# Chunk-selected attention with a gated MLP: score tiles of two PSUM banks, and one shared PSUM pool

## The chip, the core and the metric

The kernel runs on one core of one Trainium2 chip. The metric is device time in microseconds, the median of several executions. The engines are TensorE (PE, with PEld for its weight loads), VectorE (DVE), ScalarE (ACT), GpSimd (POOL) and SyncE (SP, which here only issues DMAs). PE writes to PSUM, a memory of eight banks; a bank holds 512 float32 columns on 128 partitions. ACT and DVE read PSUM out.

## What is computed

Four batches, eight heads, 768 positions, head dimension 64. For each query the keys are grouped into 24 chunks of 32. An upper bound of the query's score with each chunk comes from the chunk's smallest and largest key values; the six chunks with the highest bounds are kept. Masked softmax attention follows, and its output feeds an MLP with a spatial gate:

```python
k_min, k_max = np.min(k_chunks, axis=3), np.max(k_chunks, axis=3)
ub = np.sum(np.maximum(q[..., None, :] * k_min, q[..., None, :] * k_max), axis=-1)   # shapes left out
top_chunks = np.argsort(np.where(causal, ub, -1e9), axis=-1)[..., -6:]
scores = scale * np.matmul(q, k.transpose(0, 1, 3, 2))
scores = np.where(sel & causal_by_position, scores, -1e9)
attn = softmax(scores);  x = attn @ v            # then heads are joined: (4, 768, 512)
h = np.maximum(x @ w_in, 0.0);  u, v = h[..., :512], h[..., 512:]
v_n = (v - mean(v)) / np.sqrt(var(v) + 1e-06)
gated = u * (w_spatial @ v_n + b_spatial)
out = gated @ w_out
```

## The kernel before

**Units of work.** Two heads form a pair; there are 16 pairs, four to a batch. A head's lower triangle of scores, keys on partitions and queries along columns, has 21 blocks of 128 x 128. `TILES` packs them into six tiles of at most 512 columns: five full ones and one of 128. A tile is filled by one or two matmuls (L266), in batch 0 followed by one more that adds the triangular mask to the diagonal block (L269). One ACTIVATE (L271) then turns the tile into exponentials `e`, in float16, with scale and no bias. For batches 1 to 3 the mask is put on afterwards, by POOL, over the six diagonal blocks of the whole head (L278). `values` (L289) multiplies the 21 blocks of `e` with v, which has a column of ones appended, into one accumulator bank; `normalise` (L296, L297) divides by the sum.

**Preparation of a pair.** It happens one to two pairs ahead. PE transposes the keys (`k_transpose`, L170) into a PSUM tile kTp. DVE reduces it to chunk maxima and minima (L178, L182) and copies it into the operand `kh` (L194). kTp stays taken until the second of these copies. The queries are transposed (L205) and split into positive and negative parts `rq` by two DVE instructions (L210, L214). Eleven matmuls (L219, L222) make the bounds `ub`. Ten MAX8 instructions (L232) and one comparison (L237) turn them into selection columns, written beside the queries; `ub` stays taken until the comparison. The queries with these columns are transposed once more (L251), copied out by ACT or, early on, by DVE (L257), for the first eight pairs. For the later ones a DMA transposes them.

**The MLP.** It works on one batch while the next one's attention runs. Groups of four or six matmuls of 512 columns (L388) fill one bank each: 24 groups v, read by ACT (L398) and followed by statistics (L400) and a normalisation (L412) on DVE; 24 groups u, read by ACT (L420); 24 groups s, read by DVE (L427); 24 groups o, read by ACT (L437) and stored. Six transposed tiles of w_spatial, wtr, are copied out once by DVE (L369).

**Banks.** All eight are given out: three to the pool `ps_sc` (score tiles), one to `ps_tr`, one to `ps_acc` (the accumulator of `values`), three to `ps_ml`. `ps_ml` holds MLP groups, kTp and wtr, and in batch 0, when no MLP runs yet, the transposes of queries, selections and attention output (trm in the profile). In later batches these transposes go to `ps_tr` (tr in the profile). `ub` is always in `ps_tr`.

**Order.** A table of beats, twelve to a pair, lists which step comes when. The functions are called in that order, and the language's scheduler fixes each engine's queue from it, the data and the free buffers. Each engine then runs its own queue strictly in order. An instruction that waits for a semaphore holds up all that stand behind it on its engine. Only about the first pair and a half are ordered by hand on PE.

Of the kernel before, what the change touches and what calls it, by code (L numbers as in the profile page):

```python
# [10 lines left out]
F32 = mybir.dt.float32  # L11
F16 = mybir.dt.float16
Alu = mybir.AluOpType
Act = mybir.ActivationFunctionType
AX = mybir.AxisListType

P = 128
# [6 lines left out]
TILES = [  # L24
    [(0, 0, 512, 0)],
    [(1, 128, 512, 0)],
    [(2, 256, 512, 0)],
    [(3, 384, 384, 0), (1, 640, 128, 384)],
    [(4, 512, 256, 0), (0, 512, 256, 256)],
    [(5, 640, 128, 0)],  # L30
]
# [17 lines left out]
def kernel(  # L49
# [11 lines left out]
    nc = tc.nc  # L61
    B, H, S, D = q.shape
# [10 lines left out]
    scale = 1.0 / math.sqrt(D)  # L73
    mm = nc.tensor.matmul
# [2 lines left out]
    ring = ctx.enter_context(tc.tile_pool(name="ring", bufs=1))  # L77
    sb = ctx.enter_context(tc.tile_pool(name="sb", bufs=2))
    ml = ctx.enter_context(tc.tile_pool(name="ml", bufs=2))
    ps_sc = ctx.enter_context(tc.psum_pool(name="ps_sc", bufs=3))  # L80
    ps_tr = ctx.enter_context(tc.psum_pool(name="ps_tr", bufs=1))
    ps_acc = ctx.enter_context(tc.psum_pool(name="ps_acc", bufs=1))
    ps_ml = ctx.enter_context(tc.psum_pool(name="ps_ml", bufs=3))

# [11 lines left out]
    def at(beat, fn, *args):  # L96
        beats[beat].append((fn, args))
# [9 lines left out]
    identity = cp.tile([P, P], F16)  # L107
    tri = cp.tile([P, P], F16)
# [48 lines left out]
    class Pair:  # L157
# [37 lines left out]

        def trans_tile(self):

            if self.b == 0:
                return ps_ml.tile([P, S], F16, tag="mlp", name="trm")
            return ps_tr.tile([P, S], F16, tag="tr", name="tr")  # L200

        def q_transpose(self):
            self.tr = self.trans_tile()
# [11 lines left out]
                                        op0=Alu.mult, op1=Alu.max)  # L215

        def bounds(self):
            ub = self.ub = ps_tr.tile([P, 512], F32, tag="tr", name="ub")
            mm(ub[:, 0:(NQT - 1) * W], lhsT=sub_chunk, rhs=later, start=True, stop=False)  # L219
            for qi in range(1, NQT):  # L220
                for m in range(2):
                    mm(ub[:, (qi - 1) * W:qi * W], lhsT=self.rq[:, m, qi * P:(qi + 1) * P],  # L222
                       rhs=self.km[:, m].rearrange("p h c -> p (h c)"), start=False, stop=(m == 1 and qi == NQT - 1))
# [36 lines left out]
        def scores(self, hi, g):  # L260
            if g == 0:
                self.e[hi] = sb.tile([P, EW], F16, tag="e", name="e", bufs=3)
            self.sc = sc = ps_sc.tile([P, 512], F32, tag="sc", name="sc")
            for si, (t, q0, n, col) in enumerate(TILES[g]):
                diag = self.b == 0 and si == 0
                mm(sc[:, col:col + n], lhsT=self.kh[hi][:, t * P:(t + 1) * P],  # L266
                   rhs=self.a[:, q0 // P:(q0 + n) // P, hi, :], start=True, stop=not diag)
                if diag:
                    mm(sc[:, 0:P], lhsT=identity, rhs=tri, start=False, stop=True)  # L269
            width = sum(n for (_, _, n, _) in TILES[g])  # L270
            nc.scalar.activation(out=self.e[hi][:, g * 512:g * 512 + width], in_=sc[:, 0:width], func=Act.Exp, scale=scale)  # L271

        def triangle(self, hi):
            if self.b == 0:
# [198 lines left out]
    for g in range(1, NPAIR // 2):  # L473
        t0 = 2 * g * BEATS
# [4 lines left out]
    for i, p in enumerate(pairs):  # L479
        t0 = i * BEATS  # L480
        for hi in range(2):
            for g in range(len(TILES)):
                at(t0 + 6 * hi + g, p.scores, hi, g)
            at(t0 + 6 * hi + 6, p.triangle, hi)
            at(t0 + 6 * hi + 6, p.values, hi, LOWER[0], True)
            at(t0 + 6 * hi + 8, p.values, hi, LOWER[1])
            at(t0 + 6 * hi + 10, p.values, hi, DIAG, False, True)
            at(t0 + 6 * hi + 11, p.normalise, hi)
        at(t0 + 18, p.x_transpose)
    for i, p in enumerate(pairs):  # L490
        t0 = i * BEATS
# [20 lines left out]
    p, n = pairs[0:2]  # L512
# [82 lines left out]
```

## Time and profile before

Three runs took 208.97, 209.21 and 209.23 us; the median is 209.21. The profiled span is 206.9 us, with the TensorE clock granted in full throughout.

| what | before |
|---|---|
| ACTIVATE e<-sc, 128x512 | 160, mean 605 ns |
| ACTIVATE e<-sc, 128x128 | 32, mean 290 ns |
| MATMUL mlp, 128x512 | 432, mean 379 ns |
| MATMUL sc, all widths | 256, and 48 mask matmuls |
| MATMUL acc, 128x65 | 672, mean 193 ns |
| first matmul, last matmul | 5.7 us, 202.6 us |
| first exponential, last exponential | 15.3 us, 167.1 us |
| first MLP matmul | 55.1 us |

Matmuls are pipelined: the mean of one is the time from its start to its modelled end, while the next one starts much earlier. A row that says "x24" with a duration covers a run of neighbours, and from such rows the distance of two starts can be had. Busy shares of ACT and DVE are sums of the time in which at least one of the engine's instructions was under way. In tables of stretches a line gives the busy time and the number of instructions of PE, PEld, DVE, ACT and POOL in this order. In lists of waits the three numbers are the total in us, how many times, and the longest.

### The profile page before, as it was taken

The numbers are of one execution on the slowest core, as the hardware profiler recorded it, in microseconds if no ns is written. First come the engines' busy times: TensorE is split into PE (matmuls) and PEld (weight loads), VectorE is DVE, ScalarE is ACT, GpSimd is POOL, SyncE is SP. The second block draws the span as 40 slices with busy tenths as digits, with TensorE's granted clock in tenths as the row PEclk, the third lists the DMA queues.
The fourth block names the chain that finished last, engine by engine and source line by source line (L and its number), as shares of the span: only waits on it lengthen the run. The fifth ranks groups of instructions, "written<-read, shape, count | busy, mean of one in ns | idle before, by whom it ended". The sixth has DMA issues, their size and how long they took to land.

```text
span 206.9 us, 5068 instructions
## 1 busy us (share of the span) xinstructions
PE 187.8 (91%) x1922; PEld 115.1 (56%) x1922; DVE 154.5 (75%) x454; ACT 158.1 (76%) x326; POOL 80.5 (39%) x100
## 2 busy tenths in 40 slices
PE   0368999898899999999999999999999999999992
PEld 0266776775666665656655656565555454444440
DVE  6467979989799989899797999887647456365520
ACT  4797989899998889785989996669999830666042
POOL 7997659596992463236114111111111110000000
PEclk9999999999999999999999999999999999999999
DMA  5999999999999999979998926648782124540356
GB/s 38 92 118 154 140 178 158 173 177 167 177 162 162 97 119 128 135 130 147 149 278 153 180 62 57 127 88 158 181 166 65 38 29 92 187 152 3 72 128 256
DMA packets 114424, 27.27 MB, mean 132 GB/s; under 512 B 109536, under 2 KB 110816, under 8 KB 114400
## 3 DMA queue, kind: packets, MB, share of 16 engines
q0 software_dynamic: 76544, 12.20, 89.8%
q1 hardware_dynamic: 37856, 14.75, 36.4%
q8 instruction: 15, 0.25, 0.5%
q14 instruction: 9, 0.07, 0.1%
HBM read 24.38 MB, written 6.29 MB: 148 GB/s over the span
## 4 chain that ended last, share of the span: by engine, by line
PE 69%; ACT 17%; DVE 8%; issue 2%; DMA 2%; POOL 0%; DVEq 0%; ACTq 0%; POOLq 0%
PE mlp L388 40%; PE sc L266 12%; ACT e L271 10%; PE acc L289 7%; PE kTp L170 2%; ACT a L257 2%; DVE kmm L178 2%; PE ub L222 2%; DMA k<-in_k_dram 2%; PE trm L251 2%; ACT vraw L398 1%; PE tr L205 1%; DVE vn L412 1%; DVE kmm L182 1%; ACT u L420 1%
## 5 line engine op out<-in xcount | busy, mean ns | idle before, releaser
L271 ACT ACTIVATE e<-sc 128x512 f16<-128x512 f32 x192 | 96.9, 553 | 14.8 <-PE sc L266 13.4
L266 PE MATMUL sc<-a,kh 128*128 128x512 f16 (+3 forms) x256 | 65.5, 308 | 2.1 <-ACT e L271 1.5
L388 PE MATMUL mlp<-w_in_sb,xT 128*128 128x512 f16 x192 | 53.0, 379 | 0.1
L278 POOL TENSOR_SCALAR_AFFINE_SELECT e<-e 128x768 f16<-128x768 f16 x24 | 20.9, 869 | 66.3 <-ACT e L271 66.3
L289 PEld LDWEIGHTS <-e 128*128 128x128 f16 x672 | 31.4, 97 | 17.0 <-DVE x L297 3.8
L388 PE MATMUL mlp<-vn,wsT 128*128 128x512 f16 x144 | 37.3, 379 | 0.0
L289 PE MATMUL acc<-vt,e 128*128 128x65 f16 x672 | 35.3, 193 | 0.7 <-DVE x L297 0.4
L266 PEld LDWEIGHTS <-kh 128*128 128x128 f16 x256 | 22.7, 98 | 13.3 <-issue 0.8
L437 ACT COPY o<-mlp 128x512 f32<-128x512 f32 x24 | 14.1, 586 | 19.5 <-PE mlp L388 19.1
L400 DVE BATCH_NORM_STATS2 stats<-vraw 128x6 f32<-128x512 f32 x24 | 16.6, 693 | 12.9 <-ACT vraw L398 12.5
L388 PE MATMUL mlp<-w_out_sb,gT 128*128 128x512 f16 x96 | 25.1, 379 | 0.0
L388 PEld LDWEIGHTS <-xT 128*128 128x128 f16 x192 | 17.2, 97 | 12.6 <-issue 0.4
L427 DVE SCALAR_TENSOR_TENSOR g<-mlp,b_col,u 128x512 f16<-128x512 f32 x24 | 17.9, 748 | 7.3 <-PE mlp L388 6.2
L232 DVE MAX8 max<-ub 128x8 f32<-128x8 f32 (+4 forms) x160 | 15.6, 165 | 5.1 <-PE ub L222 4.9
L388 PEld LDWEIGHTS <-wsT 128*128 128x128 f16 x144 | 12.9, 98 | 10.4
L178 DVE TENSOR_REDUCE kmm<-kTp 128x24 f16<-128x768 f16 x16 | 15.2, 948 | 3.7 <-PE kTp L170 2.7
L297 DVE TENSOR_TENSOR x<-acc,rec 128x384 f16<-128x384 f32 x32 | 17.6, 551 | 0.4
L336 POOL DMA_DIRECT2D qs<-in_q_dram x14 | 14.6, 1049 | 5.9 <-PE sc L266 5.9
L194 DVE COPY kh<-kTp 64x768 f16<-64x768 f16 x30 | 16.5, 549 | 0.5
L398 ACT ACTIVATE vraw<-mlp 128x512 f32<-128x512 f32 x24 | 14.4, 601 | 3.0 <-PE mlp L388 3.0
L420 ACT ACTIVATE u<-mlp 128x512 f16<-128x512 f32 x24 | 14.3, 598 | 1.7 <-PE mlp L388 1.5
L327 POOL DMA_DIRECT2D k<-in_k_dram x14 | 14.4, 1045 | 2.5 <-PE kTp L170 1.8
(67 smaller groups left out, 230.2 us busy)
## 6 DMA issues: line engine op xcount, KB each, us to landing
out_dram<-o SPq DMA_DIRECT2D x24, 256.0 KB, 2.3
vt<-in_v_dram POOLq DMA_DIRECT2D x8, 384.0 KB, 8.8
k<-in_k_dram POOLq DMA_DIRECT2D x14, 192.0 KB, 8.1
qs<-in_q_dram POOLq DMA_DIRECT2D x14, 192.0 KB, 7.5
ws_raw<-in_moe_w_spatial_dram POOLq DMA_DIRECT2D x6, 192.0 KB, 6.9
w_in_sb<-in_moe_w_in_dram POOLq DMA_DIRECT2D x8, 128.0 KB, 6.9
w_out_sb<-in_moe_w_out_dram POOLq DMA_DIRECT2D x4, 128.0 KB, 7.9
k<-in_k_dram POOLq DMA_DIRECT2D x4, 96.0 KB, 3.4
```

Source lines behind the costliest of these rows:

```text
L178: nc.vector.tensor_reduce(self.kmm[:, 0, :], self.kT.rearrange("d (c ch) -> d c ch", ch=CHUNK), axis=AX.X, op=Alu.max)
L194: copy(self.kh[hi][d0:d1], self.kT[d0:d1])
L266: mm(sc[:, col:col + n], lhsT=self.kh[hi][:, t * P:(t + 1) * P], rhs=self.a[:, q0 // P:(q0 + n) // P, hi, :], start=True, stop=not diag)
L271: nc.scalar.activation(out=self.e[hi][:, g * 512:g * 512 + width], in_=sc[:, 0:width], func=Act.Exp, scale=scale)
L278: nc.gpsimd.affine_select(out=blk, in_=blk, compare_op=Alu.is_ge, fill=0.0, base=0, channel_multiplier=-1, pattern=[[0, NQT], [1, P]])
L289: mm(self.av[:, qi, :], lhsT=self.e[hi][:, c:c + P], rhs=self.v[hi][:, t, 0:D + 1], start=first and n == 0, stop=last and n == len(blocks) ...
L297: nc.vector.tensor_tensor(self.x16[:, :, hi, :], in0=self.av[:, :, 0:D], in1=rec.to_broadcast([P, NQT, D]), op=Alu.mult)
L388: mm(st[group][:, 0:cols], lhsT=lhsT, rhs=rhs, start=(j == 0), stop=(j == n - 1))
L398: nc.scalar.activation(st["vraw"][:, ti, :], h, func=Act.Relu)
L400: nc.vector.bn_stats(stats, st["vraw"][:, ti, :])
L420: nc.scalar.activation(st["u"][:, ti, :], h, func=Act.Relu)
L427: nc.vector.scalar_tensor_tensor(g, in0=vs, scalar=b_col[:, ti:ti + 1], in1=st["u"][:, ti, :], op0=Alu.add, op1=Alu.mult)
```

## The change

The three score banks and the bank of `ps_tr` become two score tiles of two banks each. A score tile takes two neighbouring entries of `TILES`, so that a head has three of 1024, 1024 and 640 columns, and one ACTIVATE reads both banks. The pool `ps_tr` is gone: `ub` and all the transposes take turns in `ps_ml` with kTp, wtr and the MLP. The aim is to issue half as many exponentials, each with one fixed cost, without using more than eight banks. The values matmuls keep their beats; the score tile g is now called at beat 2g of its head instead of g.

```diff
-    ps_sc = ctx.enter_context(tc.psum_pool(name="ps_sc", bufs=3))
-    ps_tr = ctx.enter_context(tc.psum_pool(name="ps_tr", bufs=1))
+    ps_sc = ctx.enter_context(tc.psum_pool(name="ps_sc", bufs=2))
     ps_acc = ctx.enter_context(tc.psum_pool(name="ps_acc", bufs=1))
     ps_ml = ctx.enter_context(tc.psum_pool(name="ps_ml", bufs=3))
...
         def trans_tile(self):
 
-            if self.b == 0:
-                return ps_ml.tile([P, S], F16, tag="mlp", name="trm")
-            return ps_tr.tile([P, S], F16, tag="tr", name="tr")
+            return ps_ml.tile([P, S], F16, tag="mlp", name="trm")
...
         def bounds(self):
-            ub = self.ub = ps_tr.tile([P, 512], F32, tag="tr", name="ub")
+            ub = self.ub = ps_ml.tile([P, 512], F32, tag="mlp", name="ub")
...
         def scores(self, hi, g):
             if g == 0:
                 self.e[hi] = sb.tile([P, EW], F16, tag="e", name="e", bufs=3)
-            self.sc = sc = ps_sc.tile([P, 512], F32, tag="sc", name="sc")
-            for si, (t, q0, n, col) in enumerate(TILES[g]):
-                diag = self.b == 0 and si == 0
-                mm(sc[:, col:col + n], lhsT=self.kh[hi][:, t * P:(t + 1) * P],
-                   rhs=self.a[:, q0 // P:(q0 + n) // P, hi, :], start=True, stop=not diag)
-                if diag:
-                    mm(sc[:, 0:P], lhsT=identity, rhs=tri, start=False, stop=True)
-            width = sum(n for (_, _, n, _) in TILES[g])
-            nc.scalar.activation(out=self.e[hi][:, g * 512:g * 512 + width], in_=sc[:, 0:width], func=Act.Exp, scale=scale)
+            sc = ps_sc.tile([P, 1024], F32, tag="sc", name="sc")
+            width = 0
+            for half, part in enumerate(TILES[2 * g:2 * g + 2]):
+                for si, (t, q0, n, col) in enumerate(part):
+                    col += 512 * half
+                    diag = self.b == 0 and si == 0
+                    mm(sc[:, col:col + n], lhsT=self.kh[hi][:, t * P:(t + 1) * P],
+                       rhs=self.a[:, q0 // P:(q0 + n) // P, hi, :], start=True, stop=not diag)
+                    if diag:
+                        mm(sc[:, col:col + P], lhsT=identity, rhs=tri, start=False, stop=True)
+                    width += n
+            nc.scalar.activation(out=self.e[hi][:, g * 1024:g * 1024 + width], in_=sc[:, 0:width], func=Act.Exp, scale=scale)
...
         for hi in range(2):
-            for g in range(len(TILES)):
-                at(t0 + 6 * hi + g, p.scores, hi, g)
+            for g in range(len(TILES) // 2):
+                at(t0 + 6 * hi + 2 * g, p.scores, hi, g)
```

## The prediction

> **What bounds the kernel now.** I read the page's engine line first, then a table of stretches, the waits, the order of time, and the groups by shape.
>
> ```profile
> PE 187.8 (91%) x1922; PEld 115.1 (56%) x1922; DVE 154.5 (75%) x454; ACT 158.1 (76%) x326; POOL 80.5 (39%) x100
> ```
>
> TensorE leads, but the average hides two regimes. The table of stretches (busy us of PE, PEld, DVE, ACT, POOL) splits them:
>
> ```profile
> 20.00:40.00 20.00, 18.55 (x281) 14.13 (x280) 18.41 (x61) 17.92 (x38) 13.71 (x22) 1.00 2.50 162
> 40.00:60.00 20.00, 17.85 (x257) 13.01 (x256) 17.63 (x56) 19.19 (x43) 17.28 (x21) 1.00 1.92 170
> 60.00:80.00 20.00, 19.39 (x233) 12.85 (x231) 18.99 (x60) 17.45 (x37) 10.72 (x11) 1.00 1.98 130
> 80.00:140.00 60.00, 60.00 (x632) 36.40 (x631) 53.61 (x159) 48.68 (x107) 15.21 (x16) 1.00 1.19 136
> ```
>
> Until about 78 us no engine is full: ACT leads at 40 to 60 (19.2 of 20), DVE at 60 to 80 (19.0), the two are level at 20 to 40. From 80 on PE is full and ACT is not (48.7 of 60). A busy PE need not be at its peak, so I checked its starts. In the timeline four MLP matmuls take 1.03 us and one 0.379, so the pitch is 0.217 us; a transpose's is 0.056, a values matmul's 0.030 (21 take 0.81). By such pitches the gaps between starts sum to 10.0 us from 20 to 80 us, and to 1.1 us from 80 until the end of PE at 203, of which one wait is 0.5. **After 80 us the kernel is TensorE back to back: nothing ACT saves there can shorten it, and each new PE stall there lengthens it one for one.** The waits of PE after 78 us agree; this is the whole list:
>
> ```profile
> PE acc L289 <- DVE x L297: 0.4, 1, 0.4
> ```
>
> By shape, the exponentials (busy, mean ns, idle before):
>
> ```profile
> L271 ACT ACTIVATE e<-sc 128x512 f16<-128x512 f32 x160 | 91.6, 605 | 14.8 <-PE sc L266 13.4 <-PE sc L269 0.7
> L271 ACT ACTIVATE e<-sc 128x128 f16<-128x128 f32 x32 | 9.3, 290 | 0.0
> ```
>
> And how long a bank stays taken after its last matmul, from the timeline:
>
> ```profile
> 197.67 5.34 PE L388 MATMUL mlp<-w_out_sb,gT 128*128 128x512 f16 x24
> ...
> 198.73 0.58 ACT L437 COPY o<-mlp 128x512 f32<-128x512 f32 x1 [8.04 <-PE mlp L388]
> ```
>
> The first group's fourth matmul starts at 197.67 + 3 x 0.217 = 198.32 and its copy ends at 199.31: a lag of 0.99 us on an idle ACT. Taken the same way for all groups from 78 to 166 us, the lag of a bank read by ACT is 1.00 to 1.46 (medians 1.06 to 1.12); read by DVE at L427, 1.17 to 1.92 (median 1.45); a score tile, median 1.02; the bound tile ub, 1.6 to 4.5 (median 2.7); a kT tile, 5.5 to 9.9.
>
> **The Trainium skill.** "ScalarE: Activation LUTs", What ACT_TABLE_LOAD costs: with immediate scale and bias an ACTIVATE costs 186 ns plus 0.833 ns a column, and neighbours overlap by about 93 ns. The trace agrees: (605 - 290) / 384 = 0.82 ns a column and 185 ns fixed; back to back, four take 2.09 us, so the pitch is (2.09 - 0.605) / 3 = 0.495, an overlap of 110 ns. "PSUM — Partial Sum Buffer", The four PSUM rules: one matmul writes at most one bank, so a 1024-column tile still takes two or more matmuls; "Advanced Engine Details and Errata", The Read-Write Bubble: trn2 can read several banks with one instruction. No run here has shown that yet. "Perfetto Trace Analysis", Matmuls: independent groups should rotate through banks so that reading one out overlaps the next. The trace agrees: MLP groups do so without a gap.
>
> **The change, part by part.**
>
> 1. Fewer exponentials. Per head six (five of 512, one of 128) become three (1024, 1024, 640): 192 become 96. Columns stay. What goes is the part of the pitch that isn't columns, 0.495 - 0.82 x 0.512 = 0.075 us, three times a head: 0.225 a head, 7.2 us of ACT in all. (The fixed 185 ns would give 17.8, but 110 of them overlap already.) Matmuls stay 1922, with the same pitches: 0. On the path lies only what falls before 78 us: 85 of the exponentials, 14 heads, at most 14 x 0.225 = 3.2 us. DVE, whose work is unchanged, has 55.0 of 60 us filled from 20 to 80 and is the fuller engine in two of the three rows, so I take 40% of it: **-1.3 us** (bounds 0 and -3.2). The 18 heads after that save 4.1 us of an ACT with 11 us of idle in 80 to 140: 0.
>
> 2. Score buffers: three of one bank become two of two. Two 1024 tiles hold more, but in coarser steps. In batch 0 each half takes a score and a mask matmul, 0.216 + 0.056; two halves plus about 0.4 us until a result is read is 0.95, and the other tile's exponential lasts 0.92 at its pitch. Before, 0.27 + 0.4 stood against two pitches, 0.99. The slack of 0.3 us is gone; any other PE work between halves shows on ACT. This is the second reason for 40%.
>
> 3. Banks. ps_tr's bank goes away; transposes of every batch and ub now share ps_ml's three with kT and the MLP. Mean banks held in before (last reader's end minus first matmul, summed, over the stretch): 20 to 55 us, kT 1.13 + transposes 0.93 + ub 0.57 = 2.63 of four; 55 to 78, MLP 1.10 + kT 1.00 + ub 0.45 + transposes 0.44 + wtr 0.43 = 3.42 of four; 78 to 166, MLP 1.36 + kT 0.49 + ub 0.25 + transposes 0.13 = 2.23. Now three serve. A PE wait on a bank blocks everything behind it in PE's one queue: scores, so ACT, and values, so DVE.
>
> The built order of instructions shows where. For each PE wait I added the PE pitches between the last matmul that its releaser's engine had waited for and the waiting matmul: the time PE can fill before it must stall. The coarse order is the same (at head 32 both have issued 280 of 432 MLP matmuls), but the distances shrink. Between 50 and 140 us of PE work (about 74 to 165 us on the clock), waits on a bank read by ACT with under 1.1 us: **before 1, after 11** (0.83, 0.84, 0.87, 0.88, 0.89, 0.89, 0.98, 1.05, 1.06, 1.08, 1.08). On a bank read at L427 with under 1.35: before 0, after 5 (1.10, 1.22, 1.31, 1.31, 1.33). After an L369 copy: before 1.53, after 0.71 and 0.92. Shortfalls against median lags: ACT at 1.08, 1.4; three of these evictions stand right behind a 1024 exponential, 0.42 longer than before, less what they had to spare, 1.0; L427 at 1.45, 1.0; L369 at 1.25 (its median), 0.9; score tiles, lag 1.02 + 0.42 for 1024 and + 0.10 for 640 columns against 1.01, 1.22 and 0.92, 0.8. Sum 5.1. They aren't wholly additive, since one stall lengthens the next distance and a third stand within 2 us of another; I take three quarters, less the 0.2 that before had there: **+3.7 us** (bounds 0.8 with every lag at its shortest 1.00, and 5.1). As a check the rule on before: its one ACT distance of 0.83 should stall 0.25, and the timeline has a gap of 0.235 there.
>
> 4. The same between 36 and 50 us of PE work (59 to 74 us). ACT distances 0.76, 0.76, 0.83, 0.85, 0.93 against 0.98, 0.98 before: 1.3 - 0.2; L369 distances 0.71, 0.75, 0.85 against 0.73: 1.4 - 0.5. Sum 2.0, but DVE is 19.0 of 20 full there and hides about half: **+1.0 us** (0.3 to 3.2; the upper end is 3.42 - 3 = 0.42 banks too few, 14% of 23 us).
>
> Sum: -1.3 + 3.7 + 1.0 = +3.4, so 209.2 + 3.4 = **212.6 us**. The tail from 166 us on keeps its three MLP banks and distances of 1.94 and more: 0.
>
> **Rivals.** (a) Faster: ACT's saving is real time until 78 us and evictions are prompt: -3.2 + 0.8 + 0.3 gives **207.1**. For it: ACT's 19.2 of 20 at 40 to 60. Against: DVE at 19.0 next to it. (b) A draw: -2 + 1.5 + 0.5, **209.2**. (c) Banks become the bound: nothing gained early, 3.2 lost in 55 to 78 and all 5.1 later: **217.5**. For it: 3.42 banks wanted of three. Against: part of that 3.42 is tiles waiting for a reader.
>
> **Chances.** My forecast 0.5, (a) 0.2, (b) 0.1, (c) 0.2. The range cuts half of (a) and half of (c): 207.2 to 217.0. Forecast and (c) are slower, with a little of (b): 0.71; the draw within 0.2% 0.06; faster 0.23.
>
> **What would show it.** L271: 64 of about 1.02 us and 32 of 0.71, ACT busy down by about 7 to 9 us: part 1. PE waiting for ACT and DVE at L388, L310 and the transposes between 80 and 166, where it had 0.4 us: part 3. ACT idle before 78 us, waiting for L266: part 2. A PE without gaps from 80 on, and an earlier 80, would prove me wrong, and rival (a) right.

## The result and the profile after

The changed kernel takes **215.97 us** (median of five, 215.73 to 218.33) against 209.21 us (five, 208.82 to 209.54): a ratio of 1.0351, 95% interval 1.0306 to 1.0397. That is 6.8 us more, where the prediction said 3.4 more. The direction was right and the time lies in the range; the size was half of what came.

The profiled execution was the slowest of the five, 218.33 us. An unchanged control, `after_again`, was profiled at 216.11 us, and its readings are used unless the first profile is named. Its engine line, and its exponentials by shape (busy us, mean ns, idle before):

```profile
PE 190.7 (89%) x1922; PEld 116.0 (54%) x1922; DVE 155.3 (72%) x454; ACT 151.2 (71%) x230; POOL 81.4 (38%) x100
```

```profile
L271 ACT ACTIVATE e<-sc 128x1024 f16<-128x1024 f32 x64 | 64.2, 1023 | 12.7 <-PE sc L266 9.4 <-PE sc L269 1.6 <-POOL e L278 1.1
L271 ACT ACTIVATE e<-sc 128x640 f16<-128x640 f32 x32 | 22.6, 707 | 8.2 <-PE sc L266 6.6 <-PE sc L269 1.5
```

The change does what it says: 96 exponentials instead of 192, ACT busy for 151.2 us instead of 158.1. But these fewer instructions stand behind 20.9 us of idle ACT (12.7 + 8.2), where before it was 14.8 us. Most of what ACT saved, it waits for. The stretches of the control, in the columns of the prediction's table:

```profile
20.00:40.00 20.00, 17.35 (x270) 13.57 (x269) 17.27 (x57) 16.54 (x22) 13.86 (x22) 1.00 2.49 162
40.00:60.00 20.00, 17.23 (x257) 13.13 (x254) 16.36 (x59) 17.61 (x26) 16.31 (x20) 1.00 1.92 170
60.00:80.00 20.00, 18.57 (x211) 12.06 (x210) 18.25 (x49) 16.32 (x28) 9.90 (x10) 1.00 1.48 116
80.00:140.00 60.00, 58.07 (x590) 34.36 (x589) 51.81 (x156) 43.77 (x69) 16.00 (x18) 1.00 1.12 128
```

PE lost time in every stretch: 18.55 became 17.35 in the first, and the full 60.00 from 80 to 140 us became 58.07. Its matmuls per stretch fell too (632 to 590 in the last). PE's waits from 80 us on, where before had a single one of 0.4 us (total, times, longest), again in the control:

```profile
PE sc L266 <- ACT e L271: 0.7, 2, 0.4
PE mlp L388 <- ACT u L420: 0.6, 3, 0.3
PE sc L266 <- DMA a<-qs: 0.3, 1, 0.3
PE mlp L388 <- ACT o L437: 0.3, 1, 0.3
```

These are the MLP's banks read out by ACT (L420, L437), as the forecast had it, score tiles, and one wait for a DMA that transposes queries (a<-qs). None is long. One of them in the control's timeline (start us, us, instruction, idle before):

```profile
105.76 0.58 ACT L437 COPY o<-mlp 128x512 f32<-128x512 f32 x1
...
106.40 1.02 PE L388 MATMUL mlp<-w_in_sb,xT 128*128 128x512 f16 x4 [0.26 <-ACT o L437]
```

The copy that frees the bank ends at 106.34. The group that needs it starts at 106.40, and PE has stood for 0.26 us. The list of waits holds only the longer ones (1.9 us in all). The sum of all gaps between PE's starts, by the pitches of the prediction, tells the whole:

| PE gaps, us | before 20 us | 20 to 80 | from 80 | last matmul at |
|---|---|---|---|---|
| before | 8.93 | 9.97 | 1.13 | 202.6 |
| control of after | 9.65 | 13.06 | 4.97 | 210.1 |
| difference | +0.7 | +3.1 | +3.8 | +7.5 |

The differences add up to 7.6 us, and the last matmul came 7.5 us later. So the whole loss is PE standing still, half of it before 80 us and half after.

The first profile also had one long wait. Its timeline at 54 us, and the clock line of its page (40 slices of 5.4 us):

```profile
54.33 1.42 POOL L343 DMA_DIRECT2D vt<-in_v_dram  x1 [0.74 <-PE trm L248]
...
55.80 0.86 POOL L278 TENSOR_SCALAR_AFFINE_SELECT e<-e 128x768 f16<-128x768 f16 x1
...
56.72 0.52 PE L289 MATMUL acc<-vt,e 128*128 128x65 f16 x6 [2.15 <-POOL e L278]
```

```profile
PEclk9999999999799999999999999999999999999999
```

GpSimd issues a load of v (L343) before it masks a head's exponentials (L278); the mask starts 1.47 us later, and PE waits 2.15 us for it. In before the two stood the other way round (the mask at 52.93, the load at 53.74). The clock fell in the same slice. In the control the same wait is 0.5 us and the clock stays at 1.00, and its time is 2.2 us shorter. Hence all but 0.5 us of this wait is part of the slowest execution, not of the 6.8 us.

### The profile page after: what moved, and what is told of

The parts are those of the page before. It is cut to its first block, busy times and chain, and to the rows that moved or that the text cites. A ratio compares the mean times of both kernels' runs of the same rounds, so it can differ in the third digit from the quotient of the medians.

```text
span 216.6 us, 4975 instructions
## 1 busy us (share of the span) xinstructions
PE 191.4 (88%) x1922; PEld 116.0 (54%) x1922; DVE 155.2 (72%) x454; ACT 151.2 (70%) x230; POOL 81.4 (38%) x100
## 4 chain that ended last, share of the span: by engine, by line
PE 67%; ACT 15%; DVE 6%; DMA 5%; issue 3%; POOL 3%; POOLq 0%; ACTq 0%; DVEq 0%
PE mlp L388 41%; PE sc L266 11%; ACT e L271 10%; PE acc L289 6%; DMA a<-qs 3%; PE kTp L169 2%; DMA qs<-in_q_dram 2%; PE ub L219 2%; PE trm L248 2%; PE trm L202 1%; ACT u L420 1%; DVE kmm L177 1%; ACT vraw L398 1%; ACT a L254 1%; DVE kmm L181 1%
## 5 line engine op out<-in xcount | busy, mean ns | idle before, releaser
L271 ACT ACTIVATE e<-sc 128x1024 f16<-128x1024 f32 (+1 forms) x96 | 85.6, 918 | 23.1 <-PE sc L266 18.2
L266 PE MATMUL sc<-a,kh 128*128 128x512 f16 (+3 forms) x256 | 55.8, 309 | 4.2 <-ACT e L271 3.4
L388 PE MATMUL mlp<-w_in_sb,xT 128*128 128x512 f16 x192 | 50.6, 380 | 1.2 <-ACT vraw L398 0.4
L278 POOL TENSOR_SCALAR_AFFINE_SELECT e<-e 128x768 f16<-128x768 f16 x24 | 21.0, 874 | 66.9 <-ACT e L271 66.8
L289 PEld LDWEIGHTS <-e 128*128 128x128 f16 x672 | 30.6, 98 | 17.2 <-DVE x L297 2.5
L388 PE MATMUL mlp<-vn,wsT 128*128 128x512 f16 x144 | 35.6, 379 | 0.3 <-ACT u L420 0.3
L437 ACT COPY o<-mlp 128x512 f32<-128x512 f32 x24 | 14.0, 585 | 21.8 <-PE mlp L388 21.3
L266 PEld LDWEIGHTS <-kh 128*128 128x128 f16 x256 | 21.8, 98 | 12.7 <-issue 3.6
L388 PEld LDWEIGHTS <-xT 128*128 128x128 f16 x192 | 17.7, 98 | 18.5 <-issue 3.6
L388 PE MATMUL mlp<-w_out_sb,gT 128*128 128x512 f16 x96 | 24.1, 379 | 0.0
L427 DVE SCALAR_TENSOR_TENSOR g<-mlp,b_col,u 128x512 f16<-128x512 f32 x24 | 18.0, 749 | 8.4 <-PE mlp L388 7.0
L388 PEld LDWEIGHTS <-wsT 128*128 128x128 f16 x144 | 13.1, 97 | 13.2 <-issue 1.2
L343 POOL DMA_DIRECT2D vt<-in_v_dram x8 | 11.5, 1438 | 16.6 <-PE sc L266 11.0
L420 ACT ACTIVATE u<-mlp 128x512 f16<-128x512 f32 x24 | 14.3, 598 | 4.4 <-PE mlp L388 4.2
L336 POOL DMA_DIRECT2D qs<-in_q_dram x14 | 15.2, 1093 | 3.8 <-PE trm L248 1.8
```

The source lines that it names most:

```text
L271: nc.scalar.activation(out=self.e[hi][:, g * 1024:g * 1024 + width], in_=sc[:, 0:width], func=Act.Exp, scale=scale)
L278: nc.gpsimd.affine_select(out=blk, in_=blk, compare_op=Alu.is_ge, fill=0.0, base=0, channel_multiplier=-1, pattern=[[0, NQT], [1, P]])
L289: mm(self.av[:, qi, :], lhsT=self.e[hi][:, c:c + P], rhs=self.v[hi][:, t, 0:D + 1], start=first and n == 0, stop=last and n == len(blocks) ...
L388: mm(st[group][:, 0:cols], lhsT=lhsT, rhs=rhs, start=(j == 0), stop=(j == n - 1))
L420: nc.scalar.activation(st["u"][:, ti, :], h, func=Act.Relu)
L427: nc.vector.scalar_tensor_tensor(g, in0=vs, scalar=b_col[:, ti:ti + 1], in1=st["u"][:, ti, :], op0=Alu.add, op1=Alu.mult)
```

## Experiments

All were timed beside the kernel before on the same chip. Its median was 208.7 to 208.8 us everywhere. Intervals are 95%.

### Which part costs: from before to after in four steps

**`share4_narrow`** merges the pools and leaves all else, so that the shared pool keeps all four banks and the score tiles stay at 512 columns.

```diff
-    ps_tr = ctx.enter_context(tc.psum_pool(name="ps_tr", bufs=1))
-    ps_ml = ctx.enter_context(tc.psum_pool(name="ps_ml", bufs=3))
+    ps_ml = ctx.enter_context(tc.psum_pool(name="ps_ml", bufs=4))
...
+            return ps_ml.tile([P, S], F16, tag="mlp", name="trm")
...
+            ub = self.ub = ps_ml.tile([P, 512], F32, tag="mlp", name="ub")
```

> The kernel before with only the pools merged: score tiles stay three of 512 columns, the bank of ps_tr is added to ps_ml, which has four and takes ub and all transposes. Theory banks (three banks are too few for all that shares them): none of the waits on an MLP bank between 50 and 140 us of PE work is shorter than 1.1 us here, so PE should be without gaps from 80 us on, as before: 209 us, within 1. Theory wide tiles (the coarse score tiles cost the time): also 209. Theory sharing (long-lived kT and ub in the same pool as the MLP is what hurts, however many banks): 212 or more.

Measured: 209.99 us, ratio 1.0051 (1.0032 to 1.0071).

**`share3_sc3`** is the same with three banks in the shared pool; one bank of PSUM is left unused. **`share3_sc4`** gives that bank to the score tiles.

```diff
-    ps_ml = ctx.enter_context(tc.psum_pool(name="ps_ml", bufs=4))   # of share4_narrow
+    ps_ml = ctx.enter_context(tc.psum_pool(name="ps_ml", bufs=3))   # share3_sc3, share3_sc4
-    ps_sc = ctx.enter_context(tc.psum_pool(name="ps_sc", bufs=3))
+    ps_sc = ctx.enter_context(tc.psum_pool(name="ps_sc", bufs=4))   # share3_sc4 alone
```

> Narrow score tiles in three banks and one shared pool of three: it differs from the kernel with the shared pool of four by one bank and nothing else (one of the eight banks is unused). Theory banks: that one bank brings back the gaps, 4 us or more after 80 us and 1 to 3 before: 213 to 215.5, at least 3.5 over the 210.0 of the pool of four. Against it: within 1 of 210. And if the fourth score bank mattered in the kernel with four score banks (214.5), this one is slower than that by over 0.7.

Measured: 214.53 us, ratio 1.0276 (1.0254 to 1.0298).

> The change without the wide tiles: score tiles of 512 columns and 192 exponentials, but in four banks, with the accumulator and the shared pool of three as in the changed kernel. Theory banks: 12 short waits as in the changed kernel, so 4 us of PE gaps from 80 us on, and a total of 213 to 216. Theory wide tiles: 209 to 210.

Measured: 214.54 us, ratio 1.0277 (1.0253 to 1.0301). A fourth score bank is worth nothing.

**`wide_2exp`** is after with an exponential for each bank of a score tile: coarse tiles, but 192 exponentials as before.

```diff
-            nc.scalar.activation(out=self.e[hi][:, g * 1024:g * 1024 + width], in_=sc[:, 0:width], func=Act.Exp, scale=scale)
+            for c0, c1 in ((0, 512), (512, width)):
+                nc.scalar.activation(out=self.e[hi][:, g * 1024 + c0:g * 1024 + c1], in_=sc[:, c0:c1], func=Act.Exp, scale=scale)
```

> The changed kernel with its wide tiles and pools, but two exponentials for each wide tile (512 and the rest): 192 instead of 96. It shows what the halved count is worth. Theory banks: the same gaps from 80 us on; before 80 us ACT has 14 x 0.225 = 3.2 us more to do, of which some is idle anyway: 216 to 219. If the count is worth nothing: 216.0, within 0.7. Theory wide tiles (a wide exponential holds up the reading of MLP banks): faster than 216, since an eviction waits for half an exponential at most: 213 to 215.

Measured: 216.13 us, ratio 1.0358 (1.0334 to 1.0382).

**`after_again`** is after, unchanged.

> The changed kernel again, unchanged, as a control: 216.0, within 0.5. Its first profile was of the slowest of five executions. If the wait of 2.1 us for the mask at 54 us and the dip of PE's clock beside it belong to that execution, they are absent or much smaller here, and the gaps between PE's starts from 20 to 80 us sum to 13 to 14 us instead of 15.8; those from 80 us on stay at 5.3, within 0.5.

Measured: 215.88 us, ratio 1.0349 (1.0305 to 1.0393).

By the ratios, times 208.7 us, the steps are: merging the pools +1.1, one bank fewer in the shared pool **+4.7** (4.5 by the medians), the fourth score bank 0, tiles of two banks **+1.7**, and half as many exponentials **-0.2**, less than the intervals can tell from nothing. The step to tiles of two banks also moves the calls of the scores to other beats. The gaps of PE say where:

| PE gaps, us | before 20 us | 20 to 80 | from 80 |
|---|---|---|---|
| before | 8.93 | 9.97 | 1.13 |
| share4_narrow | 9.11 | 11.35 | 1.89 |
| share3_sc3 | 8.96 | 13.21 | 3.78 |
| share3_sc4 | 8.7 | 12.7 | 4.2 |
| wide_2exp | 8.99 | 13.15 | 5.25 |
| after_again | 9.65 | 13.06 | 4.97 |

Each row is one profile. That of `share4_narrow` is of its slowest execution, 210.81 us against a median of 209.99, so its gaps are some 0.8 us too large for the step: the table makes merging look dearer and the bank cheaper than the times do. And 1.2 us of `wide_2exp`'s gaps from 80 us on are one wait for a transposing DMA (a<-qs), which takes 0.6 in `share3_sc4` and 0.3 in the control: part of what the coarse tiles cost there is no wait for a bank.

PE's waits from 80 us on in `share4_narrow`, then in `share3_sc3`:

```profile
PE sc L263 <- DMA a<-qs: 0.5, 1, 0.5
PE acc L286 <- DVE x L294: 0.2, 1, 0.2
```

```profile
PE sc L263 <- ACT e L268: 0.4, 1, 0.4
PE acc L286 <- DVE x L294: 0.4, 1, 0.4
PE mlp L385 <- ACT u L417: 0.2, 1, 0.2
```

(In kernels without the lines of `ps_tr`, line numbers are up to three lower: L385 and L417 are L388 and L420 of before.) With four shared banks no MLP group is in the list, with three one is. Most of the difference is in gaps too short for it: by the gaps over 60 ns, MLP groups wait 1.72 us from 80 us on in `share3_sc3`, and none in `share4_narrow`.

**`wide_tr_ml2`** tests the rival that sharing, not the number of banks, is the harm: after with transposes and `ub` in a bank of their own again, and two banks for the rest.

```diff
+    ps_tr = ctx.enter_context(tc.psum_pool(name="ps_tr", bufs=1))
...
-    ps_ml = ctx.enter_context(tc.psum_pool(name="ps_ml", bufs=3))
+    ps_ml = ctx.enter_context(tc.psum_pool(name="ps_ml", bufs=2))
...
-            ub = self.ub = ps_ml.tile([P, 512], F32, tag="mlp", name="ub")
+            ub = self.ub = ps_tr.tile([P, 512], F32, tag="tr", name="ub")
```

> The changed kernel with wide tiles, but ub and the later transposes get their own bank again, and ps_ml has two. Theory banks: 18 short waits instead of 11, PE gaps from 80 us on of 6 us or more, a total of 217 to 222. Theory sharing: with ub and tr out of the MLP's pool, 210 to 213.

Measured: 218.55 us, ratio 1.0472 (1.0445 to 1.0499), 2.6 us slower than after. Gaps from 80 us rise to 7.45. The sharing theory falls: of the same three banks, sharing is the better use.

### Is it the bank, or a worse order of instructions?

Every change of pools also makes the scheduler plan another queue. The next four kernels take the planner away for PE: its queue is the order of the calls. They are slower as a whole, and are compared with each other. `fixed_before`, `fixed4`, `fixed3` and `fixed_after` are before, `share4_narrow`, `share3_sc3` and after with this edit; in the first three all 1922 matmuls stand in the same order. The queues of ACT and DVE are still planned, and differ a little.

```diff
-    for beat in sorted(beats):
-        for fn, args in beats[beat]:
-            fn(*args)
+    with tc.manual_schedule(engines={mybir.EngineType.PE}):
+        for beat in sorted(beats):
+            for fn, args in beats[beat]:
+                fn(*args)
```

> The kernel before with PE's queue in the order of the calls; ps_tr is a bank of its own. The order is that of fixed4. If merging the pools costs nothing by itself: within 0.7 of fixed4. If the 1.3 us by which the planned kernel with the pool of four is slower than before come from sharing and not from the plan: 1 to 1.5 faster than fixed4.

> Narrow tiles, one shared pool of four, and PE's whole queue in the order in which the functions are called (the scheduler doesn't move PE's instructions). Its own level is not known, since the planned order may be better or worse; it is the base for the three beside it.

> The same with a shared pool of three. PE's instructions stand in the same order, all 1922 matmuls. Theory banks (waits): the short waits that appear between 36 and 140 us of PE work, 0.22, 0.61, 0.71, 0.77, 0.77 on ACT's banks, 0.61, 0.77, 1.26, 1.26 on L427's and 0.06 on L369's, fall short of the median lags by 5.4 us, three quarters of it 4: fixed4 + 3 to + 6. Theory plan (the other order is what costs): fixed4 + 0 to + 1.5.

> The changed kernel with PE's queue in the order of the calls. Against fixed3 it has wide tiles (64 + 32 exponentials) in four score banks. Theory coupling: slower than fixed3 by 1 to 4 us, with PE waiting longer for L271. If fewer exponentials help once the order is given: faster than fixed3 by 1 to 3.

| kernel | us | ratio to before | step | gaps 20 to 80 | gaps from 80 |
|---|---|---|---|---|---|
| fixed_before | 224.48 | 1.0773 (1.0722 to 1.0824) | | 18.42 | 8.07 |
| fixed4 | 224.09 | 1.0738 (1.0699 to 1.0777) | -0.4 | 18.04 | 8.59 |
| fixed3 | 229.14 | 1.0992 (1.0950 to 1.1034) | +5.05 | 19.14 | 12.17 |
| fixed_after | 232.25 | 1.1134 (1.1106 to 1.1161) | +3.1 | 19.89 | 14.14 |

PE's waits from 20 us to the end in `fixed4` (the first two lines, and the only one at the MLP), and the first eight in `fixed3`:

```profile
PE acc L286 <- DVE x L294: 10.5, 16, 1.6
PE acc L286 <- POOL e L275: 3.7, 1, 3.7
...
PE mlp L385 <- DVE wsT L366: 0.3, 1, 0.3
```

```profile
PE acc L286 <- DVE x L294: 7.7, 12, 1.4
PE trm L307 <- DVE x L294: 2.6, 3, 1.3
PE wtr L365 <- DVE qs L234: 1.7, 1, 1.7
PE kTp L169 <- DVE rq L211: 1.3, 1, 1.3
PE mlp L385 <- DVE g L424: 1.2, 2, 0.9
PE mlp L385 <- ACT vraw L395: 1.0, 2, 0.7
PE mlp L385 <- DVE wsT L366: 0.9, 1, 0.9
PE ub L216 <- DVE wsT L366: 0.9, 1, 0.9
```

The accumulator's waits (acc) are the price of the fixed order, and are smaller with three banks. What is new in `fixed3` are waits of tiles of the shared pool (wtr, kTp, mlp, ub) for readers of *other* tiles of that pool: a transpose of w_spatial waits until DVE has done with `ub` (L234), a bound until a copy of wtr is out (L366). In the whole lists the waits at tiles of that pool grow by some 9 us, and those at the accumulator shrink by 6. With the same order of PE, **one bank costs 5.05 us**: the loss is waiting, not a worse plan of PE. (That ACT's and DVE's new plans have no part in it isn't shown.)

Merging costs nothing in a fixed order. So the +1.1 of `share4_narrow` is most likely its new plan; that is by exclusion, and `fixed4` is a shaky base for small steps. Its profile holds a wait of 3.7 us for a mask, again behind a load of v, and the clock was granted by half for 6.8 us; in `fixed3` this lasted 3.4 us, and in `fixed_before` and `fixed_after` it didn't happen before PE's last matmul. Half of 6.8 and of 3.4 us bounds what this cost PE, so I estimate the error of a step at 1 to 3 us. It makes the bank's 5.05 too small rather than too large; from 80 us on, where both had the full clock, the bank's step in the gaps is 3.6 us (8.59 to 12.17).

From `fixed3` to `fixed_after` the order of the calls changes with the tiles, so that its +3.1 holds both. Its waits at the MLP, and at the selections' transposes:

```profile
...
PE trm L248 <- ACT a L254: 2.2, 3, 1.2
...
PE mlp L388 <- DVE g L427: 1.9, 3, 0.9
PE mlp L388 <- ACT u L420: 1.9, 2, 1.4
```

More time is lost at banks of the shared pool that ACT reads, less at the score tiles: by the gaps from 20 to 80 us, 0.91 in `fixed3` and 0.16 in `fixed_after`. That fits evictions queued behind exponentials of 1.02 us instead of 0.605, a link that is argued from the durations and that no run isolates.

### Do coarse score tiles cost by themselves?

**`mixed_tiles`** keeps before's `ps_tr` and `ps_ml` and turns its three score banks into one tile of two and one of one, taken in turn: 128 exponentials.

```diff
-    ps_sc = ctx.enter_context(tc.psum_pool(name="ps_sc", bufs=3))
+    ps_sc = ctx.enter_context(tc.psum_pool(name="ps_sc", bufs=1))
+    ps_sn = ctx.enter_context(tc.psum_pool(name="ps_sn", bufs=1))
...
+            wide = g in (0, 3)
+            sc = ps_sc.tile([P, 1024], F32, tag="sc", name="sc") if wide else ps_sn.tile([P, 512], F32, tag="sn", name="sc")
...
-            for g in range(len(TILES)):
+            for g in (0, 2, 3, 5):
```

> The kernel before, all pools as they were, but the three score banks are used as one tile of 1024 columns and one of 512 in turn: four exponentials a head (1024, 512, 1024, 128), 128 in all, and no bank lost elsewhere. It asks what fewer exponentials bring when nothing is paid in banks. ACT is spared 2 x 0.075 a head, 2.1 us for the 14 heads before 80 us. Theory ACT bound before 80 us: 207.5 to 208.5. Theory coupling (in coarse steps PE and ACT wait for each other, which eats the saving): 209 to 212, with PE waiting for L271 longer than the 1.5 us of before between 20 and 80 us.

Measured: 213.88 us, ratio 1.0247 (1.0204 to 1.0290). PE's waits for score tiles from 20 to 80 us in it, and then in before:

```profile
PE sc L271 <- ACT e L276: 6.1, 12, 0.8
```

```profile
PE sc L266 <- ACT e L271: 1.5, 5, 0.7
```

The lists hold the longer waits; with the short ones counted, PE stands 8.3 us there for exponentials, against 4.9 in before. With the shared banks untouched and a third fewer exponentials, the kernel is 5.1 us slower, more than either expectation had. Three banks as two buffers cost more than they save. Two things change at once here, the size of the tiles and their number (two instead of three), and no run separates them.

### Did ACT set the pace before 80 us, or DVE?

**`lean_act`** is before, with half the columns exponentiated in batch 0 (the rest of `e` is preset to ones by DVE at the start, in three buffers of its own, so the output isn't the reference's). It takes some 8.8 us from ACT.

```diff
+            nc.vector.memset(t[:, 0:2560].rearrange("p (g c) -> p g c", c=512)[:, :, 256:512], 1.0)
...
+            if self.b == 0:
+                width //= 2
             nc.scalar.activation(out=self.e[hi][:, g * 512:g * 512 + width], in_=sc[:, 0:width], func=Act.Exp, scale=scale)
```

> The kernel before, but in batch 0 each exponential reads and writes only half of its columns (the other half of e is set to ones once, so the output differs). ACT is spared 1344 x 0.82 ns = 1.1 us a head, 8.8 us in all between 15 and 58 us, nearly three times what halving the count can spare it before 80 us. If ACT sets the pace there: 205 or less. If ACT only takes turns with DVE and PE, as I now believe since halving the count brought nothing: 207.5 to 209. The memsets may cost up to 1 us at the start.

Measured: 212.85 us, ratio 1.0198 (1.0183 to 1.0214). ACT's waits from 15 to 80 us, and the stretches 20 to 60:

```profile
ACT a L263 <- PE trm L257: 4.7, 5, 1.9
ACT e L279 <- PE sc L272: 2.7, 3, 1.6
ACT er L279 <- PE sc L275: 2.4, 7, 0.5
```

```profile
20.00:40.00 20.00, 17.78 (x266) 13.55 (x264) 17.51 (x62) 13.42 (x41) 13.04 (x21) 1.00 2.47 156
40.00:60.00 20.00, 17.02 (x258) 12.57 (x256) 16.75 (x52) 15.51 (x37) 15.65 (x20) 1.00 1.83 172
```

ACT is busy for 28.9 of 40 us instead of 37.1, and idles for its inputs. The presetting makes the start some 3 us late (the values of head 1 end at 24.0 instead of 20.9 us), so the total, outside both expectations, is no measure. But from there to head 10 it takes 37.6 us, against 36.9 in before. **An ACT relieved of a fifth of its work didn't shorten the stage.** So its 19.2 of 20 us were not by themselves the bound. The scheduler also ordered PE's queue somewhat differently (as it did in `lean_dve`), and what that cost is not known.

**`lean_dve`** is before without the chunk minima of the first eight pairs (a 24-column copy of 0.15 us in place of each reduction of 0.95 us; the selection is another one). DVE is busy for 148.7 us instead of 154.5.

```diff
+            if self.i < 8:
+                nc.vector.tensor_copy(self.kmm[:, 1, :], self.kT[:, 0:NCH])
+                return
```

> The kernel before without the minimum over the key chunks for the first eight pairs (a copy of 24 columns stands in its place, so the selection differs). DVE is spared 8 x 0.85 us = 6.8 us, most of it before 80 us. If DVE sets the pace there: 205 or less. If no one engine does: 207 to 208.7.

Measured: 208.18 us, ratio 0.9980 (0.9969 to 0.9990). The last of these copies is at 53 us, so all the relief lies before that. And there it comes through in part: head 9 ends 2.3 us earlier than in before (51.9 against 54.2), and PE's gaps from 20 to 55 us are 6.7 instead of 8.2. The lead is lost right after: at head 14 (81 us), at head 20 and at the end it is 0.5 us, and the gaps from 55 to 80 us are 3.2 instead of 1.9. Over both, 20 to 80, they are 9.88 against 9.97. So DVE has a share in the pace up to 55 us. From there to 80 us neither run relieves anything, and there the lead is used up.

PE's gaps show how waits trade places. In before, 4.9 of its 10.0 us from 20 to 80 us end with an exponential that frees a score tile. `share3_sc4`, with a fourth score bank, has 2.3 us of this kind where `share3_sc3` has 5.5, and is no faster: the other gaps grow. No single engine, and no single pool, sets the pace up to 55 us.

### Two smaller questions

**`after_v4`** gives after a fourth buffer for v, so that the load at L343 need not stand where it delays the mask.

```diff
-    v_ring = [ring.tile([P, 4, NQT, D + 2], F16, name=f"vt{i}") for i in range(3)]
+    v_ring = [ring.tile([P, 4, NQT, D + 2], F16, name=f"vt{i}") for i in range(4)]
...
-        t = v_ring[g % 3]
+        t = v_ring[g % 4]
```

> The changed kernel with four buffers for v instead of three. In the changed kernel a load of v stands ahead of a triangular mask in GpSimd's queue and waits for PE at 54 us; PE then waited 2.1 us for that mask. With a fourth buffer the load waits for older work. Theory GpSimd queue: 213.5 to 214.5. Theory banks: this wait was of the profiled execution, the slowest of five, and what it hid comes back as waits for banks: 215.3 to 216.3.

Measured: 215.24 us, ratio 1.0301 (1.0283 to 1.0319): 0.6 us less by the medians, with intervals that overlap the control's. At most a small part of the loss is GpSimd's queue.

**`before_kearly` and `after_kearly`** copy both halves of the keys out of kTp right after its reductions, so that this bank, the longest held (for a median of 7.2 us after its last matmul in the control, 6.1 with the edit), comes free sooner. If the *mean* number of banks held were what counts, after should gain.

```diff
-        at(t0 - 15, p.k_operand, 0)
+        at(t0 - 19, p.k_operand, 0)
...
-        at(t0 - 11, p.k_operand, 1)
+        at(t0 - 19, p.k_operand, 1)
```

> The changed kernel with both copies out of kT placed right after the chunk minimum, so that a kT tile gives its bank back sooner, after about 4 us instead of 7.6. Nothing else is changed, the pool keeps three banks. Theory mean banks held (2.6 and 3.4 wanted of three): 213 to 214.5. Theory short distances (what counts is how few matmuls the built order puts between the last one of a bank's owner and the first of the next): the built order still has 10 waits under 1.1 us on ACT's banks and 5 under 1.35 on L427's, so 215 to 216.3.

> The kernel before with both copies out of kT placed right after the chunk minimum. Its built order has none of the short waits between 50 and 140 us of PE work, as before nearly, but six under 1.0 us between 36 and 50 where before had two. Theory short distances: 208.5 to 209.7. If the time that kT holds a bank matters before 80 us: 206.5 to 208.

Measured: `after_kearly` 215.40 us, ratio 1.0338 (1.0299 to 1.0376), no different from after. That speaks against the mean, though here too PE's order is a new one. `before_kearly` 212.54 us, ratio 1.0200 (1.0153 to 1.0246), a miss for both theories: 3.9 us slower, 3.4 of it in PE's gaps from 20 to 80 us (13.35). One piece of it, from its waits of PE at 55 to 80 us:

```profile
PE acc L289 <- POOL e L278: 1.8, 1, 1.8
```

That is a load of v ahead of a mask again, in a kernel with all its banks. An edit of two beats changed the queues by as much as the dearest part of the change under study did. The rest of the 3.9 us was not traced.

## Why the prediction was half right

**Part 3, the bank waits from 80 us on: right in kind and in the total, not in its pieces.** Forecast +3.7, measured +3.8 (gaps 1.13 to 4.97). By what ended them, the control's gaps of over 30 ns there are these, beside three quarters of the forecast's pieces:

| gaps from 80 us, us | forecast | control |
|---|---|---|
| shared banks read by ACT, with those behind long exponentials | 1.8 | 2.3 |
| shared banks read by DVE at L427 and L369 | 1.4 | 0.5 |
| score tiles, waiting for an exponential | 0.6 | 1.1 |
| a transposing DMA (a<-qs) | none | 0.5 |
| accumulator | none | 0.2, before 0.8 |

The close total owes something to luck. DVE's banks came free sooner than taken: the lag at L427 is 1.22 us in the control (median), where 1.45 was taken. For ACT's banks it is 1.06 to 1.26, about as taken; the score tile's grew from 1.02 to 1.28, less than the + 0.42 taken for the wide ones, yet PE waited longer for them. The rule itself, distance in PE's queue against lag of the reader, did well once more with PE's order held: it had put `fixed3` 3 to 6 us above `fixed4`, and 5.05 came.

**Part 1, ACT's saving, failed: "I take 40% of it: -1.3 us".** The size of the saving was right (7.2 us computed, 6.9 measured), what it is worth was not: -0.2 by `wide_2exp` against the control, that is with three shared banks. The step behind it was that ACT, at 19.2 of 20 us, leads the stage from 40 to 60 us, so that a share of its relief lies on the path. `lean_act` speaks against it: with a fifth of ACT's work gone, the stage was no shorter. That PE, ACT and DVE hold the pace together, as a loop in which each waits for tiles of the others, fits all the runs but is a reading. "Perfetto Trace Analysis" in the Trainium skill (Identifying the Most-Contended Engine) says to optimise the engine with the highest occupancy first; in this stretch that was ACT, at 19.2 of 20 us, and relieving it brought nothing: the measurement disagrees.

**Part 4, waits before 80 us, failed in its size: "DVE is 19.0 of 20 full there and hides about half: +1.0 us".** Measured +3.1 from 20 to 80 us. From 55 to 80 us, which holds the forecast's 59 to 74, PE's gaps grew by 2.4 us (1.9 to 4.3 in the control), and the distances had given 2.0 before they were halved. So the failed step is the halving. In before PE itself had only these 1.9 us of gaps in 25 us; it was about as full as DVE, and a new stall had little to hide behind. This last is a reading of the trace and not a test. A second step failed with it: before 55 us, where on average 2.63 of the three banks left were wanted, the forecast counted no waits at all, and the gaps grew by 0.6 us from 20 to 55 and by 0.7 before 20. The ladder splits the 3.1 into 1.4 for merging and 1.9 for the bank, with the doubt about `share4_narrow`'s profile told above; that the new plan of a merged pool would cost anything by itself was not in the forecast.

**Part 2, coarser tiles, had no number of its own.** It served as a reason to halve part 1, and a piece of it was in part 3. Measured, it is +1.5 to +1.7 in after, and in the gaps most of that lies after 80 us (4.2 in `share3_sc4`, 5.25 in `wide_2exp`, with 0.6 of it for the DMA named above). In `mixed_tiles` it is 5.1.

So the forecast had -0.3 before 80 us and +3.7 after; the gaps show +3.8 and +3.8. The whole error lies before 80 us. There, rival (c) was nearer: it gained nothing early and lost 3.2. Of the signs named, exponentials of 1.02 and 0.71 us and ACT's drop came, the waits at L388 came, ACT's idle time before L266 came; no waits of PE at L310 or the transposes over the list's threshold from 80 us on.

**Open:** what sets the pace before 80 us: up to 55 us relieving ACT brought nothing and relieving DVE some 2 us, from 55 to 80 no run relieved an engine, and GpSimd, busy for 17.3 of 20 us from 40 to 60 in before, was relieved in none; how the cost of coarse tiles splits between later evictions and score tiles that come free late; and how much of the first 20 us' +0.7 is more than the scatter of one profile. Nothing here points to a version faster than before: each part of the change costs or is worth nothing, and `lean_dve` leaves work out.

## What to carry to other kernels

A high busy share over a stretch is no bound unless the engine's waits are gone too; relieve it by leaving work out, see whether the stage shortens, and only then count its savings. Look at the end too: a lead can be lost again further on. Where one pool of buffers feeds an engine's single queue, count for each wait the work between the releaser and the waiter and hold it against the reader's lag: this gave the loss after 80 us to a few tenths in total, though not engine by engine, where the mean number of buffers in use (2.23 of three) suggested none. Coarser tiles trade a small fixed cost on one engine for slack between two, and any change of buffers re-plans the queues; price both, and fix the order in a test to tell them apart.

## What the runs showed of the hardware

One ACTIVATE over two banks costs nothing extra: 1023 ns for 1024 columns and 707 for 640 give 0.82 ns a column and some 180 ns fixed, as within one bank before (0.82 and 185). This is what "Advanced Engine Details and Errata" in the Trainium skill (The Read-Write Bubble) states, that one instruction can read several banks, and no run had shown it before. Its advice there, large tiles to spread the overhead, held for ACT's busy time and not for the kernel's.

TensorE's granted clock was halved beside waits of PE in three of the profiles: in the first profile of after for 3.4 us from 56.4 us on, at the end of the wait of 2.15 us; in `fixed4` for 6.8 us from 59.1 on, at a wait of 3.7; in `fixed3` for 3.4 us from 34.9 on, at two waits of 1.3 and 1.4 within 3 us. It stayed at 1.00 in `fixed_after` at a wait of 2.1 us (71 us), in `before_kearly` at one of 1.8 (55 us), and in `fixed_before` at the same two waits of 1.3 and 1.4 us as in `fixed3`. So the length of a wait doesn't decide it alone; what else does is open.
